# Keys turned by VectorE in square blocks and spread through DRAM, their product with V in three column tiles, from unit 3 on

## The chip, the cores and the metric

The kernel runs on one core of one Trainium2 chip (trn2). The metric is the device time of one execution in microseconds (us), lower is better. Five engines work side by side, each through its own instructions in their order: TensorE (PE; its weight loads are listed apart as PEld), VectorE (DVE), ScalarE (ACT), GpSimd (POOL) and SyncE (SP), which here issues all DMAs.

## The reference

Two stages stand one after the other. The first is linear attention with a complex decay per channel: for each of 4 batches and 8 heads a state S of 48 x 48 is carried over 768 time steps. The second takes the 3072 tokens of 384 numbers that come out and applies a two-layer network with the activation h * tanh(softplus(h)).

```python
B, H, S, D = 4, 8, 768, 48
for t in range(S):
    new_re = ar * S_re - ai * S_im
    new_im = ar * S_im + ai * S_re
    kv = np.einsum('bhd,bhe->bhde', k[:, :, t], v[:, :, t])
    S_re, S_im = (new_re + kv, new_im)
    y[:, :, t] = np.einsum('bhd,bhde->bhe', q[:, :, t], S_re)
...
h = x @ w_in                       # 384 -> 2048
g = h * np.tanh(softplus(h))
out = g @ w_out                    # 2048 -> 384
```

## The kernel before

The work is cut into 12 units of 256 tokens (`TU`), three for each batch, and a unit into two chunks of 128 time steps (`C`). Inside a chunk the recurrence is written as matrix products: with running products of the decay, q is multiplied by the growing product and k divided by it, each as a real and an imaginary part, so that a head has 96 rows (48 cosine, 48 sine).

**Elementwise stage** (`ew_steps`, L340). ACT, DVE and a few POOL instructions make the products of a unit; `rot` and `relay` (L498 to L507) send them by 12 DMAs a chunk (`T<-X`, `T<-QK`, L502) into the tile `T`, which has 96 partitions and for each of the 8 heads q, k and the end factor over the chunk's time. Three such tiles exist (`TB`).

**Attention stage** (`chunk`, L568), for each chunk:
- `kn` (L574): the keys of `T` are needed with time on the partitions. Eight TensorE transposes of 96 x 128 (L578, `pkn<-ident,T`) write PSUM, and two ACT copies (L579) bring them into `knat` (named `kn` in the profile), one buffer of 128 partitions, where the 96 columns of a head lie together and a column of zeros closes the tile. The last chunk of a batch has none, since its state is not carried on: 20 chunks of 24 turn their keys.
- `amat` (L582): keys times queries for each head, written from unit 3 on (`PU`) in two column tiles of 64 (L596); DVE masks the result into `am` (L599, L603).
- `yv` (L614): the output of the chunk, from the old state (`ypsum<-T,S`) and from `am` with V (`ypsum<-am,V`, and `ypsum<-am,vx` for a second copy of half of V whose partitions are swapped by halves, loaded at L377). L628 copies it to `y`, and `fin` (L673) sends `y` on by DMA (L676).
- `upd` (L633): keys times V for each head (L642, `pd<-V,kn`), in two column tiles of the array, channels 0 to 63 and 64 to 96 (the 97th is the zero column); then DVE adds the old state and multiplies by the end factor (L649, L650). It is left out where `kn` is.

These matmuls take float32 operands, and each is two hardware instructions in the profile; a transpose is one.

**Network stage** (`moe_steps`, L687). A unit has 8 steps `mm1` and 8 steps `mm2`. `mm1` (L709) makes 256 columns of h with 18 matmuls; then a chain of Exp, minimum, Square, Ln, Exp (L713 to L717) and `g` (L719) follows on ACT and DVE; g is split into a high part `gh`, a copy with a narrower type (L725, booked on the helper's L294, all on DVE here), and a low part `gl` (DVE, L295). `mm2` (L746) multiplies both into two output tiles with 12 matmuls.

**Order.** The order of each engine is written out by hand in the table `ORDER` (L73), as runs of instruction numbers, and `in_order` (L205) fixes it. What an engine does next, and also in which order SP issues its DMAs, is set by this table and not by a scheduler. An SP instruction that waits for a semaphore holds up all DMAs behind it.

Of the kernel before, what the change touches and what calls it, by code (L numbers as in the profile page):

```python
# [40 lines left out]
GACT = 0  # L41
# [14 lines left out]
WQ = 768  # L56
PU = 3
LW = [-15.9, -15.8, -15.7, -15.6, 2.0, 2.5, 3.0, 3.5, -2.0, -1.5, -1.0, -0.5, 5.0, 5.5, 6.0, 6.5]
# [70 lines left out]
    """,  # L129
    "DVE": """  # L130
# [89 lines left out]
def tile_kernel(ctx, tc, q, k, v, are, aim, w_in, w_out, out):  # L220
# [77 lines left out]
    nc.vector.memset(ypsum[32:64], 0.0)  # L298

    knat = at.tile([P, 2 * D * H + 1], F32, name="kn")  # L300
    nc.gpsimd.memset(knat[:, 2 * D * H:], 0.0)

    turned = []
    masked = []
# [696 lines left out]
```

## Time and profile before

| | |
|---|---|
| median of 3 runs | 594.03 us (592.22 to 594.89) |
| profiled execution, its own time | 596.8 us |
| span of its trace | 595.1 us |
| DVE busy | 482.4 us, 81% of the span |
| ACT busy | 476.6 us, 80% |
| POOL busy | 47.6 us, 8% |
| DMA | 68.9 MB, mean 116 GB/s |

The profile counts an engine busy while at least one of its instructions runs. Matmuls overlap each other, so the time that a matmul takes from the array is read from the distance of the starts and not from its own duration. The rows on TensorE stand in the prediction.

### The profile page before, as it was taken

To read this page: it belongs to the slowest core of one execution; us is meant where nothing else is said; L and a number is where in the kernel's file an instruction comes from. 1 tells how busy PE (TensorE), PEld (TensorE's weight loads), DVE (VectorE), ACT (ScalarE), POOL (GpSimd) and SP (SyncE) were. 2 spreads that over 40 slices of the span, in tenths; PEclk is the share of its full clock that TensorE was granted. 3 is DMA by queue.
4 is the path that set the end of the run, shared out by engine and by line. 5 is a ranking of instruction groups with operands and counts; after the bars stand their busy time and mean duration, and the time that the engine had idled before them with its cause. 6 is when DMAs were issued, how large, how long until landed. Compare 5 with 4: busy or idle time off the path is not lost.

```text
span 595.1 us, 12998 instructions
## 1 busy us (share of the span) xinstructions
PE 562.9 (95%) x5134; PEld 522.0 (88%) x5134; DVE 482.4 (81%) x890; ACT 476.6 (80%) x743; POOL 47.6 (8%) x58
## 2 busy tenths in 40 slices
PE   0989899989999999999999999999999999999995
PEld 0557687879998999999999899999999999999995
DVE  6999889999999897897796798797797787564553
ACT  7999889899987998798798798688797686546651
POOL 2102213170000000000010010000010010000000
PEclk9999899999999999999999999999999999999999
DMA  8788835715525608206407206417117115001001
GB/s 294 241 271 243 280 81 161 239 41 147 164 64 122 194 8 219 83 15 161 134 14 209 53 18 172 120 54 213 42 32 206 26 48 147 1 17 39 1 15 46
DMA packets 60421, 68.91 MB, mean 116 GB/s; under 512 B 5184, under 2 KB 53952, under 8 KB 60352
## 3 DMA queue, kind: packets, MB, share of 16 engines
q1 hardware_dynamic: 60352, 68.00, 39.7%
q8 instruction: 42, 0.69, 0.5%
q14 instruction: 27, 0.22, 0.1%
HBM read 38.73 MB, written 5.51 MB: 74 GB/s over the span
## 4 chain that ended last, share of the span: by engine, by line
PE 72%; DMA 8%; ACT 8%; DVE 6%; SPq 4%; issue 2%; DVEq 0%; ACTq 0%
PE po L746 28%; PE ph L709 28%; PE ypsum L623 5%; PE pa L596 4%; DMA T<-X 3%; SPq L502 2%; PE pd L642 2%; DMA raw<-w_out 2%; ACT e L262 2%; PE pkn L578 2%; ACT X L262 2%; ACT L270 1%; DMA T<-QK 1%; PE po L742 1%; DMA raw<-w_in 1%
## 5 line engine op out<-in xcount | busy, mean ns | idle before, releaser
L709 PE MATMUL ph<-xH,w 128*128 128x256 f32 x1104 | 230.5, 288 | 3.0 <-DVE g L719 2.9
L746 PE MATMUL po<-w,gh 128*128 128x384 f32 x704 | 205.5, 341 | 0.0
L709 PEld LDWEIGHTS ph<-xH,w 128*128 128x128 f32 x1104 | 182.4, 190 | 7.1 <-issue 2.1
L709 PE MATMUL ph<-xL,w 128*128 128x256 f32 x552 | 155.5, 283 | 0.5 <-DVE xL L295 0.5
L262 ACT ACTIVATE e<-e 128x512 f32<-128x512 f32 (+1 forms) x200 | 120.0, 609 | 20.8 <-DVE e L714 18.8
L746 PEld LDWEIGHTS po<-w,gh 128*128 128x128 f32 x704 | 128.7, 188 | 2.7 <-issue 1.3
L746 PE MATMUL po<-w,gl 128*128 128x384 f32 x352 | 118.8, 338 | 0.0
L709 PEld LDWEIGHTS ph<-xL,w 128*128 128x128 f32 x552 | 104.7, 190 | 2.1 <-DVE xL L295 0.8
L262 ACT ACTIVATE e<-ph 128x512 f32<-128x512 f32 (+1 forms) x100 | 57.2, 575 | 46.6 <-PE ph L709 41.1
L719 DVE SCALAR_TENSOR_TENSOR g<-e,ph 128x512 f32<-128x512 f32 (+1 forms) x100 | 65.8, 660 | 28.9 <-ACT e L262 23.0
L262 ACT ACTIVATE e<-e,fifth 128x512 f32<-128x512 f32 (+1 forms) x100 | 70.1, 702 | 1.8
L714 DVE TENSOR_SCALAR e<-e 128x512 f32<-128x512 f32 (+1 forms) x100 | 40.9, 411 | 32.9 <-ACT e L262 32.5
L746 PEld LDWEIGHTS po<-w,gl 128*128 128x128 f32 x352 | 66.2, 188 | 0.2
L270 ACT ACT_TABLE_LOAD x47 | 60.3, 1283 | 1.6 <-PEq L957 0.8
L295 DVE TENSOR_TENSOR gl<-g,gh 128x512 fp32r<-128x512 f32 x88 | 59.8, 685 | 0.7
L294 DVE CAST gh<-g 128x512 fp32r<-128x512 f32 x88 | 36.8, 420 | 6.6 <-PE po L746 5.7
L549 PE MATMUL junk<-cmask 128*128 128x512 bf16 x84 | 22.7, 416 | 15.7 <-DVE I L465 14.8
L262 ACT ACTIVATE X<-R 128x768 f32<-128x768 f32 (+1 forms) x40 | 29.6, 759 | 8.0 <-DVE R L442 5.3
L623 PE MATMUL ypsum<-am,V 128*48 128x128 f32 x240 | 35.6, 273 | 0.3 <-DVE am L610 0.2
L623 PE MATMUL ypsum<-T,S 96*48 96x128 f32 x320 | 34.2, 275 | 0.0
L323 POOL TENSOR_TENSOR raw<-raw 128x768 int32<-128x768 int32 x16 | 26.7, 1671 | 89.3 <-ACT raw L262 34.5
L262 ACT ACTIVATE X<-X 128x768 f32<-128x768 f32 (+1 forms) x42 | 31.3, 750 | 0.3
(91 smaller groups left out, 813.8 us busy)
## 6 DMA issues: line engine op xcount, KB each, us to landing
T<-X SPq DMA_DIRECT2D x72, 129.0 KB, 2.6
T<-QK SPq DMA_DIRECT2D x72, 129.0 KB, 2.6
raw<-w_in SPq DMA_DIRECT2D x8, 768.0 KB, 7.1
raw<-w_out SPq DMA_DIRECT2D x8, 768.0 KB, 6.3
V<-v SPq DMA_DIRECT2D x12, 384.0 KB, 4.2
out_dram<-o SPq DMA_DIRECT2D x24, 192.0 KB, 2.5
I<-a_im SPq DMA_DIRECT2D x11, 384.0 KB, 4.7
R<-a_re SPq DMA_DIRECT2D x11, 384.0 KB, 5.5
```

The lines of the kernel that those rows point to most:

```text
L262: ins = nc.scalar.activation(out, in_, func, **kw)
L270: ins = nc.scalar.preload_act_table_set(name)
L294: heng(h, src)
L295: leng(out=lo, in0=src, in1=h.bitcast(F32), op=ALU.subtract)
L323: nc.gpsimd.tensor_tensor(hi, hi, lo, ALU.add)
L549: ins = nc.tensor.matmul(junk, cmask, cmask.unsqueeze(1).broadcast_to([P, 4, P]), start=True, stop=True)
L596: nc.tensor.matmul(pa[row:row + C // 2, i, hi * C // 2:], T[:, 1, hi * C // 2:][:, :C // 2], T[:, 0, hi * C // 2:C], start=True, stop=True)
L623: nc.tensor.matmul(py[64 * par:64 * par + D, i, :], lhs, rhs, start=n == 0, stop=first or n == 1)
L709: nc.tensor.matmul(ph[:, a, :], rows_in(parts[j][:, wp], kt, a), st[xp][:, kt, :], start=n == 0, stop=n == 8)
L714: nc.vector.tensor_scalar_min(e, e, math.exp(20.0))
L719: nc.vector.scalar_tensor_tensor(g, e, 2.5, ph, ALU.subtract, ALU.mult)
L746: nc.tensor.matmul(po[t], gp[:, a, tsl], rows_out(parts[NPAIR + j][:, wp], a), start=j in starts and a == 0 and n == 0, stop=j + 1 in ends ...
```

## The change

**Keys, from unit 3 on (`KU`), in the 15 chunks that carry their state on.** `kn` is replaced by two steps. `kturn` is one DVE instruction that transposes the keys of all heads in blocks of 32 x 32 into a tile of 96 partitions by 1024 numbers; this tile lies in a buffer `idle()` that it shares with `vx`. `kspread` writes that tile to DRAM with one DMA (393 KB) and reads it back with three, one for each block of 32 channels, so that time lies on 128 partitions; a run is 256 numbers, 1 KB. `knat` then holds the channels as three groups of 32, each with all heads, and is still one buffer.

**Product with V.** `upd` has three column tiles of 32 channels (24 matmuls, 48 hardware instructions) from unit 3 on, where it had tiles of 64 and 33 (16 matmuls, 32 instructions).

**`vx`** has one buffer instead of two, since the space beside it is the new tile's.

**`gh`.** From unit 2 on, the copy for the steps 1, 3, 5 and 7 (`GA`) is made by ACT (`scalar.copy`) and not by DVE: 40 copies.

**Order.** The table `ORDER` is new for all engines.

```diff
-GACT = 0
+KU = 3
+GA = (1, 3, 5, 7)
...
     "PE": """
-        0+20 40+4 48+4 44+4 52+4 20+4 56+24 24+16 80+4 124+12 84+9 136+4 188+3 93+3 156+16 191+3 226+3 248+6 229+3
...
+        0+24 40+4 48+8 44+4 56+8 24+8 64+16 32+4 124+4 36+4 128+8 80+12 188+3 226+3 92+4 248+3 191+3 229+3 136+4 251+3
...
+    spare = []
+
+    def idle():
+        if not spare:
+            spare.append(wts.tile([P, 2 * WQ], F32, tag="w", name="vx", bufs=2 * NPAIR + 1))
+        return spare[0]
...
-            if not crossed:
-                crossed.append(wts.tile([P, 2, NCH, DM], F32, tag="w", name="vx", bufs=2 * NPAIR + 1)[..., :DM // 2])
-            st["vx"] = crossed[0][:, u % 2]
+            st["vx"] = idle()[:, :NCH * DM // 2].rearrange("p (c x) -> p c x", c=NCH)
...
+            def ktile():
+                return idle()[:2 * D, NCH * DM // 2:][:, :H * C]
+
+            def kturn():
+                kt = ktile().rearrange("p (b h k) -> p h b k", b=C // 32, h=H)
+                nc.vector.transpose(kt, st["T"][c][:, :, 1, :C].rearrange("p h (b t) -> p h b t", t=32))
+
+            def kspread():
+                kd = dram.tile([2 * D, H * C], F32, name=f"kd{u}_{c}")
+                nc.sync.dma_start(kd, ktile())
+                for a in range(2 * D // 32):
+                    nc.sync.dma_start(knat[:, a * 32 * H:(a + 1) * 32 * H],
+                                      kd[a * 32:(a + 1) * 32].rearrange("p (b x) -> b p x", b=C // 32))
...
-                pd = bank([2 * D + 1, H, D], "pd", "pd", c)
+                pd = bank([2 * D + (u < KU), H, D], "pd", "pd", c)
...
-                    for lo, hi in ((0, 64), (64, 2 * D + 1)):
-                        nc.tensor.matmul(pd[lo:hi, h, :], knat[:, h * 2 * D + lo:h * 2 * D + hi], own(c, h),
+                    for lo, hi in ((0, 64), (64, 2 * D + 1)) if u < KU else ((0, 32), (32, 64), (64, 96)):
+                        at0 = h * 2 * D + lo if u < KU else lo * H + h * 32
+                        nc.tensor.matmul(pd[lo:hi, h, :], knat[:, at0:at0 + hi - lo], own(c, h),
...
-            return ([] if last else [kn(0), kn(1)]), [amat(0), amat(1)], [take, yv(0), yv(1)], [] if last else [take, upd]
+            return ([] if last else [kn(0), kn(1)] if u < KU else [kturn, kspread]), [amat(0), amat(1)], [take, yv(0), yv(1)], [] if last else [take, upd]
...
-                split(g, gh, gl, nc.scalar.copy if unit < GACT else nc.vector.tensor_copy, nc.vector.tensor_tensor)
+                split(g, gh, gl, nc.scalar.copy if 1 < unit < UNITS and j in GA else nc.vector.tensor_copy, nc.vector.tensor_tensor)
```

Three places show how the new order reads. The first is TensorE's row before, in unit 5, chunk 0: the eight transposes stand between the network's matmuls (`po`, `ph`).

```order
L746 MATMUL po<-w_1630,gh 128x384 x2
L746 MATMUL po<-w_1630,gl 128x384
L578 MATMUL pkn<-ident,T 128x96 x8
L746 MATMUL po<-w_1093,gh 128x384
L746 MATMUL po<-w_1093,gl 128x384
```

In the changed kernel no transpose stands on TensorE from unit 3 on. The same chunk's product of keys and V there has its new form, 24 matmuls of 32 channels, and is followed at once by `yv`:

```order
L723 MATMUL ph<-xL,w_984 128x256
L723 MATMUL ph<-xH,w_984 128x256
L656 MATMUL pd<-V,kn 32x48 x24
L636 MATMUL ypsum<-T,S 48x128 x2
L636 MATMUL ypsum<-am,V 48x128
L636 MATMUL ypsum<-am,vx 48x128
```

Over the whole program, from the first `mm1` of split parts on, TensorE passes 78 times between the network's matmuls and those of `amat`, `yv` and `upd` before, and 68 times after. Of the 30 ends of the 15 new `upd` runs, 20 lie against `amat` or `yv`, the others against the network's matmuls. From the start of a unit's `amat` for chunk 0 to the start of its `upd` stand between 64 (unit 8) and 180 (unit 3) matmuls of the network.

The third place is SP's row in unit 3 of the changed kernel. `kd` is the tile in DRAM (3_0 is unit 3, chunk 0), `kn` is `knat`, `T<-X` and `T<-QK` are the relays for unit 4, and `xf<-y` sends unit 3's output on.

```order
L590 DMA kd_0_1730<-vx 96x1024
L365 DMA QK<-q 128x6x128
L376 DMA vx<-v 64x2x192 x2
L592 DMA kn<-kd_0_1730 128x1x256 x3
L590 DMA kd_1_1876<-vx 96x1024
L592 DMA kn<-kd_1_1876 128x1x256 x3
L501 DMA T<-X 16x8x258 x4
L501 DMA T<-QK 16x8x258 x3
L690 DMA xf<-y 128x1x256 x2
```

The write waits for `kturn`, the reads for the write's landing and for the `upd` that last read `knat`; relays and output stand behind them in the same queue.

More of the change, by code (lines that the diff above doesn't have):

```diff
@@ L130 @@
     "DVE": """
[29 rows of a table removed]
[29 rows of a table added]
     """,
     "Activation": """
[22 rows of a table removed]
[23 rows of a table added]
     """,
     "Pool": """
-        11+2 8 1 3 13 10 0 4 2 9 14+8 24 5 23 22 25+4 7 29 6 31+3 30 34 39 35 37 36 38 40+2 54 43 42 44+4 49 48 51 50
-        53 52
+        12+2 0 8 1 11 2+3 9 5+2 14 10 15+7 23 22 24+6 7 31 33 32 54 30 35 34 36+4 41 40 42+4 47 46 48+2 51 50 52+2
     """,
     "SP": """
[11 rows of a table removed]
[13 rows of a table added]
     """,
@@ L301, in tile_kernel @@
     nc.gpsimd.memset(knat[:, 2 * D * H:], 0.0)
+    spare = []
[3 more added lines that the diff above has]
+        return spare[0]
     turned = []
     masked = []
-    crossed = []
     def load_w(n):
```

224 rows, old and new, of the table ORDER are left out of this document.

## The prediction

> **What bounds the kernel now.** I read the page's first part, then the stretches, then the order of time on TensorE.
>
> ```profile
> PE 562.9 (95%) x5134; PEld 522.0 (88%) x5134; DVE 482.4 (81%) x890; ACT 476.6 (80%) x743; POOL 47.6 (8%) x58
> ```
>
> TensorE leads, but a share of the span doesn't say in which stretch. The busy time by stretches does (columns: stretch and its length, then busy time and instructions of each engine, granted clock, DMA share, GB/s):
>
> ```profile
> 0.00:30.00 30.00, 13.93 (x102) 7.76 (x103) 24.80 (x51) 25.74 (x47) 5.06 (x16) 1.00 0.80 267
> ...
> 120.00:150.00 30.00, 28.44 (x240) 26.40 (x238) 30.00 (x49) 29.19 (x46) 10.52 (x7) 1.00 0.32 93
> 150.00:200.00 50.00, 49.60 (x470) 47.82 (x468) 46.68 (x92) 43.94 (x66) 0.89 (x5) 1.00 0.50 140
> 200.00:250.00 50.00, 50.00 (x487) 48.54 (x486) 42.09 (x76) 43.34 (x65) 1.01 (x3) 1.00 0.43 113
> 250.00:300.00 50.00, 49.39 (x512) 47.68 (x511) 41.18 (x78) 41.73 (x63) 0.64 (x2) 1.00 0.32 92
> ```
>
> From 150 us on, where units 3 and later have their attention, TensorE is busy for 49.4 to 50 of 50 us at the full clock, while DVE and ACT have 3 to 9 us to spare. So there the end is set by how much array time the instructions take, one for one, and the change takes array time away. Before 150 us DVE and ACT are nearly full too; of the change only the order and four copies of unit 2 touch that part.
>
> **Transposes removed.** The timeline around unit 5's eight transposes (start, length, instruction):
>
> ```profile
> 238.40 0.34 PE L746 MATMUL po<-w,gl 128*128 128x384 f32 x1
> 238.58 0.82 PE L578 MATMUL pkn<-ident,T 96*128 96x96 f32 x8
> 239.19 0.42 PE L746 MATMUL po<-w,gh 128*128 128x384 f32 x1
> 239.44 0.34 PE L746 MATMUL po<-w,gl 128*128 128x384 f32 x1
> ```
>
> The next matmul starts 0.61 us after them, and its successor 0.25 us later where the usual distance is 0.17 (238.40 to 238.58): 0.61 + 0.08 = 0.69 us. Fifteen chunks lose them: 15 x 0.69 = **-10.4 us**. Their 30 copies on ACT go too.
>
> **The product with V** goes from 32 to 48 hardware instructions.
>
> ```profile
> 252.72 1.07 PE L642 MATMUL pd<-V,kn 128*64 128x48 f32 x31
> 253.58 0.31 PE L623 MATMUL ypsum<-T,S 96*48 96x128 f32 x1
> ```
>
> Its groups, weight loads (PEld) apart (busy us, mean ns of one, idle before):
>
> ```profile
> L642 PE MATMUL pd<-V,kn 128*64 128x48 f32 x320 | 22.2, 223 | 0.0
> ...
> L642 PEld LDWEIGHTS pd<-V,kn 128*64 128x64 f32 x320 | 20.7, 138 | 2.8 <-issue 2.1 <-ACT e L262 0.4
> ...
> L642 PE MATMUL pd<-V,kn 128*33 128x48 f32 x320 | 19.5, 213 | 0.0
> ...
> L642 PEld LDWEIGHTS pd<-V,kn 128*33 128x33 f32 x320 | 17.7, 110 | 0.0
> ```
>
> A run takes 253.58 - 252.72 = 0.86 us, 27 ns an instruction. If instructions come one after another at that distance, 48 take 1.29 us: +0.43 a chunk, +6.5 us in all. If column tiles run beside each other (one lasts 223 ns and the next starts long before its end), each tile has 16 instructions at 0.86 / 16 = 54 ns, and a tile of 33 columns has loads of 110 ns for 138 with 64: some 28 ns less, so 16 x 26 = 0.42 us with three tiles abreast, -0.44 a chunk, -6.5 us. A third tile would have to cost nothing for that. I take the middle, **0**, by which the third tile's cost and the shorter loads cancel, and keep both ends.
>
> **Changes of width.** Going between the network's matmuls, as wide as the array, and narrow tiles costs something:
>
> ```profile
> 279.41 0.28 PE L709 MATMUL ph<-xL,w 128*128 128x256 f32 x1
> 279.53 0.28 PE L709 MATMUL ph<-xH,w 128*128 128x256 f32 x1
> 279.74 1.56 PE L596 MATMUL pa<-T 96*64 96x128 f32 x32
> 281.23 0.45 PE L746 MATMUL po<-w,gh 128*128 128x384 f32 x1
> 281.51 0.34 PE L746 MATMUL po<-w,gl 128*128 128x384 f32 x1
> ```
>
> The first narrow one comes 0.21 us after its forerunner instead of 0.12, and after the run the second wide one comes 0.28 us after the first instead of 0.17: 0.09 in, 0.11 out, 0.10 a change. The new order has 68 such changes for 78: **-1.0 us**. Against this, 20 ends of the new `upd` runs now lie against `amat` or `yv`, a change from 32 to 64 columns which the trace doesn't have; between 0 and 0.10 each, 0 to 2.0 us; I take the middle, **+1.0**.
>
> The Trainium skill, "TensorEngine Tiling (Array Packing)", section "Tiling Modes", says that another tiling mode, and not merely another tile, drains the array. The rows above agree for full width against 64 columns; for 32 against 64 no row shows it. By that rule the term would be 2.0 instead of 1.0.
>
> **What moves to other engines.**
>
> ```profile
> L294 DVE CAST gh<-g 128x512 fp32r<-128x512 f32 x88 | 36.8, 420 | 6.6 <-PE po L746 5.7
> ...
> L579 ACT COPY kn<-pkn 128x384 f32<-128x384 f32 x40 | 18.5, 470 | 6.3 <-PE pkn L578 6.2
> ...
> L442 DVE TENSOR_TENSOR_SCAN R<-rmask,R 128x768 f32<-128x768 uint8 x10 | 17.5, 1747 | 0.1
> ...
> L412 DVE TENSOR_TENSOR X<-X 128x768 f32<-128x768 f32 x10 | 9.5, 950 | 0.0
> ...
> L294 ACT CAST xH<-xf 128x768 fp32r<-128x768 f32 x11 | 9.1, 827 | 3.3 <-DMA xf<-y 3.3
> ...
> L437 DVE TENSOR_SCALAR X<-X 128x768 f32<-128x768 f32 x10 | 5.5, 552 | 0.0
> ...
> L294 ACT CAST xH<-xf 128x384 fp32r<-128x384 f32 x2 | 0.9, 507 | 0.0
> ```
>
> A copy of 512 columns on ACT lies between 507 (384 columns) and 827 ns (768): 614. ACT gains 40 x 0.614 and loses 30 x 0.470: +24.6 - 14.1 = +10.5 us, one us in a unit. DVE loses 40 x 0.420 = 16.8. A block transpose isn't in the trace; 1024 numbers a row at the rates of L437 and of L442 are 0.74 and 2.33 us, and I take the rate of L412, the commonest for one result a number: 1.27 us, fifteen times 19.0. So DVE gains 2 us. Both hide behind TensorE, which the stretches allow from 150 us on: **0**. In unit 2 four copies, 2.5 us, go onto an ACT with 29.19 of 30 us taken, while DVE, with 30.00 of 30, is relieved of 1.7: between -1.7 and +2.5, taken as 0.
>
> **The way of the keys.** No engine's time, but a wait that was not there. Rows for its steps: DMAs with KB each and us to landing, then an issue's time on SP (least, median, most ns).
>
> ```profile
> T<-X SPq DMA_DIRECT2D x72, 129.0 KB, 2.6
> ...
> V<-v SPq DMA_DIRECT2D x12, 384.0 KB, 4.2
> ...
> R<-a_re SPq DMA_DIRECT2D x11, 384.0 KB, 5.5
> ...
> held<-o SPq DMA_DIRECT2D x4, 192.0 KB, 2.5
> ```
>
> ```profile
> L377 SPq DMA_DIRECT2D vx<-v x18: 556/600/815, 174.0 to 483.8; - x18
> ```
>
> Turn 1.27, issue 0.6, write 2.5 to 5.5 (a smaller write to DRAM; a load of its size), three reads issued 1.8, the last landed 2.6 to 4.2 later (one of its size; a load of all three's): 8.8 to 13.4 us, where transposes and copies took 0.69 and 0.47. What covers it in TensorE's new order is the `amat` run (1.49 us above) and then 64 to 180 network matmuls at 0.12 (L709) or 0.17 us (L746). For chunk 0 of units 3 to 11 that sums to 27.5, 16.4, 15.3, 12.2, 13.3, 10.4, 10.9, 13.5 and 11.6 us. For the write no end is the nearer (one row has the direction, the other the size), so I take 3.9, for the reads the row of their size: 10.2 us, which just fits under all nine, **0**. At 12 us three units wait, 1.6 + 1.1 + 0.4 = 3.1 us; at 13.4 it is 8.6. For chunk 1, only the reads are left after chunk 0's `upd` has released `knat`: 1.8 + 2.6 = 4.4 us under 6.6 or more. The largest wait of SP's queue (us in total, times, longest):
>
> ```profile
> SPq L762 <- DVE o L761: 99.4, 9, 25.9
> ```
>
> Sixty added DMAs, 36 us of SP, lie in such waits; behind a waiting read the next unit's relays stand, and they are late if the array reaches the next `amat` first.
>
> **Start.** TensorE's longest wait after the first 30 us (in brackets, with what ended it):
>
> ```profile
> 63.15 0.85 PE L578 MATMUL pkn<-ident,T 96*128 96x96 f32 x8 [2.03 <-DMA T<-X]
> ```
>
> Units 0 and 1 are only reordered; I bound what that gives or takes by this wait, 2.0 us either way, and take **0**.
>
> **Sum.** -10.4 + 0 - 1.0 + 1.0 + 0 + 0 + 0 = -10.4 us. The profiled execution took 596.8 us, 1.7 more than its span, so its like would take 586.4. The median of the runs is 594.03, 0.5% under the profiled one; less 10.4 it gives **583.6 us**.
>
> **Rivals.**
> 1. *The third tile costs as the others do.* The 27 ns an instruction hold, and `upd` takes +6.5 us: 583.6 + 6.5 = 590.1. For it speaks that 32 instructions took just 27 ns each; against it, that the narrower tile's loads are shorter and that instructions overlap eightfold (223 / 27). The Trainium skill, "TensorE: Matmul & The Clock Gate", section "Back-to-back issue gap", gives a floor of about 60 cycles, some 25 ns, to a matmul of 1 to 64 columns; by it an estimate for 48 is 1.2 us a run, 588.7 in all, and the trace's 27 ns agree with it without proving it.
> 2. *Three tiles abreast.* 0.42 us a run: 583.6 - 6.5 = 577.1.
> 3. *ACT becomes the bound.* Its +10.5 us land on the path: 594.1, no change. For it: ACT is at 43.9 of 50 us, and in a chain whose steps wait for each other. Against it: from 120 to 150 us TensorE did 28.44 of 30 with ACT at 29.19.
> 4. *The keys come late: slower.* One place, `upd` of chunk 0 waiting for `knat`. If the write takes as a 384 KB load (5.5), the reads too (4.2), and `kturn` stands behind a DVE instruction of 1.75 us (L442) in the queue, the way is 13.4 + 1.7 = 15.1 us. Then units 6 to 11 miss 2.9, 1.8, 4.7, 4.2, 1.6 and 3.5 us, 18.7 in all: 602.3. It eats the gain from about 13.7 us on.
>
> **How the numbers follow.** Forecast, 579 to 589: 0.54. Rival 1: 0.14; rival 2: 0.08; rival 3: 0.11; rival 4: 0.13. A measurement of this kernel can tell about 0.5%, 3 us, from no change. Faster, under 591.1: forecast, rival 2 and two thirds of rival 1, 0.72; within 0.5%: the rest of rival 1, rival 3 and mild lateness, 0.17; slower: 0.11. The range takes in rivals 1 to 3 and leaves out most of rival 4: 577 to 597.
>
> **What would show it.** The `pd` runs of 24 matmuls: 0.86 us, or 0.42 or 1.29. No wait of TensorE for DMA `kn` over a few tenths, none of `amat` for `T`. TensorE still at 49 to 50 of 50 us from 150 us on, and the last `po` some 10 us earlier. ACT near 487 us, DVE near 484. Wrong would be a row of waits `pd` for `kn` (rival 4), or TensorE with holes after `g` (rival 3).

## The result, and the profile after

The changed kernel takes **601.44 us** (median of 4 runs, 600.37 to 603.00), the kernel before 593.91 (4 runs, 592.22 to 594.89): ratio 1.0132, 95% interval 1.0100 to 1.0164. It is slower by 1.3%. The prediction was 583.6 with a range of 577 to 597, so it was wrong by 17.8 us, in sign and beyond the range. The profiled execution took 601.4 us with a span of 599.6.

The row of TensorE from the page after, and the same stretches as before (stretch, length, busy time and instructions of each engine, granted clock, DMA share, GB/s):

```profile
PE 555.0 (93%) x5254; PEld 513.8 (86%) x5254; DVE 480.8 (80%) x865; ACT 484.3 (81%) x753; POOL 38.2 (6%) x58
```

```profile
150.00:200.00 50.00, 47.41 (x484) 45.14 (x481) 44.47 (x78) 39.05 (x61) 1.02 (x2) 1.00 0.52 150
200.00:250.00 50.00, 46.57 (x476) 44.48 (x475) 40.58 (x74) 41.81 (x62) 0.42 (x2) 0.93 0.54 148
250.00:300.00 50.00, 47.51 (x478) 46.20 (x479) 44.86 (x81) 44.30 (x68) 0.93 (x4) 0.99 0.55 147
```

Where TensorE was busy for 49.4 to 50 us it now is for 46.6 to 47.5, and the granted clock is below 1 in two of the three stretches. TensorE has holes, and its largest waits behind the start (us in total, times, longest) name them:

```profile
PE pd L656 <- DMA kn<-kd: 8.3, 9, 1.5
PE pkn L577 <- DMA T<-QK: 5.4, 3, 2.4
PE ph L723 <- DVE g L733: 2.6, 3, 1.5
PE ypsum L636 <- DVE am L616: 2.4, 1, 2.4
```

The product of keys and V waits for the keys nine times; the second row lies in the units before 3, as before. The longest hole, at 222.9 us, is the fourth row, a wait for `am` and not for keys. VectorE had `am` behind an instruction that waited for ScalarE, and ScalarE waited for the load `I` (each engine's timeline, in brackets the idle time and what ended it):

```profile
222.84 1.76 DVE L484 TENSOR_TENSOR QK<-QK,X 128x1536 f32<-128x1536 f32 x1 [5.31 <-ACT R L278]
```

```profile
218.82 0.85 ACT L258 ACTIVATE X<-I 128x768 f32<-128x768 f32 x1 [2.94 <-DMA I<-a_im]
```

SyncE issued that load at 213.40, between a chunk's first and second read; the first read had held the queue until 212.79, when the write of its keys had landed. So this hole too stands behind the keys' hold on the queue. (In the run below whose reads don't wait for their write, a hole of 2.0 us is left there, so that wait alone doesn't make it.) Around it the stretches are:

```profile
224.00:225.00 1.00, 0.00 (x0) 0.00 (x0) 0.97 (x3) 0.00 (x0) 0.00 (x0) 0.50 0.00 0
225.00:226.00 1.00, 0.70 (x6) 0.60 (x8) 0.94 (x4) 0.00 (x0) 0.00 (x0) 0.50 0.00 0
226.00:228.00 2.00, 2.00 (x13) 1.63 (x10) 1.97 (x3) 1.90 (x4) 0.00 (x0) 0.50 0.25 89
228.00:230.00 2.00, 2.00 (x8) 2.00 (x7) 1.95 (x4) 1.97 (x4) 0.00 (x0) 0.50 0.30 108
```

Within a microsecond of the stop the granted clock falls to 0.5, and it stays there after the work is back. Two such stretches, 6.83 us at 223.8 and 3.41 us at 298.9, lie behind unit 3 in the trace after, none before. Compared by the distance of neighbouring starts, class by class, from 150 us on TensorE loses some 17.1 us in waits where it lost 3.7, and 4.3 us at half clock where it lost nothing: 17.7 us more. The waits for keys (8.3 us) and the one for `am` (2.4) are most of these waits.

Other rows that answer to the prediction's, from the groups by line of the kernel after (busy us, mean ns of one, idle before):

```profile
L290 ACT CAST gh<-g 128x512 fp32r<-128x512 f32 x40 | 24.4, 611 | 7.5 <-PE po L760 5.7 <-DVE g L733 1.6
L586 DVE STREAM_TRANSPOSE vx<-T 96x1024 f32<-96x1024 f32 x15 | 18.5, 1235 | 0.3 <-DMA T<-QK 0.2
```

And the run of unit 5, chunk 0, in TensorE's timeline after:

```profile
258.17 0.28 PE L723 MATMUL ph<-xH,w 128*128 128x256 f32 x1
258.37 0.88 PE L656 MATMUL pd<-V,kn 128*32 128x48 f32 x48
259.19 0.43 PE L636 MATMUL ypsum<-T,S 96*48 96x128 f32 x4
```

The two estimates of durations, 614 ns and 1.27 us, were near (611 and 1235 ns). The run with its end takes 259.19 - 258.37 = 0.82 us with 48 instructions, where 32 took 0.86: its 48 starts lie within 0.67 us, so the tiles do run abreast.

### The profile page after: what moved, and what is told of

Its sections match the earlier page's. It is cut to its first block, busy times and chain, and to the rows that moved or that the text cites. A ratio compares the mean times of both kernels' runs of the same rounds, so it can differ in the third digit from the quotient of the medians.

```text
span 599.6 us, 13309 instructions
## 1 busy us (share of the span) xinstructions
PE 555.0 (93%) x5254; PEld 513.8 (86%) x5254; DVE 480.8 (80%) x865; ACT 484.3 (81%) x753; POOL 38.2 (6%) x58
## 2 busy tenths in 40 slices
DMA packets 68041, 80.71 MB, mean 135 GB/s; under 512 B 5604, under 2 KB 60132, under 8 KB 67972
## 4 chain that ended last, share of the span: by engine, by line
PE 45%; DMA 19%; ACT 13%; DVE 13%; SPq 5%; issue 3%; DVEq 0%; ACTq 0%
PE po L760 17%; PE ph L723 15%; DMA kn<-kd 6%; ACT e L258 5%; DMA kd<-vx 5%; PE ypsum L636 4%; ACT X L258 2%; PE pa L609 2%; SPq L501 2%; PE pd L656 2%; PE junk L548 2%; PE ph L719 2%; PE po L756 2%; ACT L266 1%; SPq L592 1%
## 5 line engine op out<-in xcount | busy, mean ns | idle before, releaser
L723 PE MATMUL ph<-xH,w 128*128 128x256 f32 x1104 | 226.7, 287 | 2.6 <-DVE g L733 2.6
L760 PEld LDWEIGHTS po<-w,gh 128*128 128x128 f32 x704 | 130.3, 190 | 3.3 <-issue 1.8
L636 PE MATMUL ypsum<-am,V 128*48 128x128 f32 x240 | 37.0, 276 | 2.8 <-DVE am L616 2.4
L548 PE MATMUL junk<-cmask 128*128 128x512 bf16 x84 | 22.7, 418 | 14.4 <-DVE I L464 14.4
L324 POOL TENSOR_TENSOR raw<-raw 128x768 int32<-128x768 int32 x16 | 28.0, 1749 | 86.9 <-DVE raw L322 25.1
L656 PEld LDWEIGHTS pd<-V,kn 128*32 128x32 f32 (+2 forms) x880 | 18.0, 115 | 14.6 <-DMA kn<-kd 8.2
```

What stands on the lines that cost most here:

```text
L324: nc.gpsimd.tensor_tensor(hi, hi, lo, ALU.add)
L548: ins = nc.tensor.matmul(junk, cmask, cmask.unsqueeze(1).broadcast_to([P, 4, P]), start=True, stop=True)
L636: nc.tensor.matmul(py[64 * par:64 * par + D, i, :], lhs, rhs, start=n == 0, stop=first or n == 1)
L656: nc.tensor.matmul(pd[lo:hi, h, :], knat[:, at0:at0 + hi - lo], own(c, h), start=not on_pe, stop=True)
L723: nc.tensor.matmul(ph[:, a, :], rows_in(parts[j][:, wp], kt, a), st[xp][:, kt, :], start=n == 0, stop=n == 8)
L760: nc.tensor.matmul(po[t], gp[:, a, tsl], rows_out(parts[NPAIR + j][:, wp], a), start=j in starts and a == 0 and n == 0, stop=j + 1 in ends ...
```

## The experiments

Theory 1: the gain is there, and the late keys take more than all of it. Rival 2: the new order, or ACT and DVE with their added work, set the end. Theories under 1 (1a to 1j) differ in what makes the keys late. Each time is a median, beside the kernel before measured with it (594 to 595 us); the ratio to it has its 95% interval in brackets.

### What the way costs, and whether SyncE's queue is at fault

**No way at all.** The DMAs of `kspread` are left out; the order is that of the changed kernel without them.

```diff
             def kspread():
-                kd = dram.tile([2 * D, H * C], F32, name=f"kd{u}_{c}")
-                nc.sync.dma_start(kd, ktile())
...
+                return
```

> The changed kernel without the 60 transfers of the keys (15 writes to DRAM, 45 reads back); the block transposes on VectorE stay. From unit 3 on the product of keys and V uses the keys that unit 2 left in its buffers, so it is not that of the reference. Theory 1, the keys come late: the 10 us of waits for keys before the product and most of the 4.4 us at half clock go, 586 to 591 us, and no row of the waits names the keys. Rival 2, the new order, or ScalarE and VectorE with their added copies, set the end: 598 to 602 us, the time at which the product waited is waited elsewhere. Between 592 and 597 both have a part.

580.3 us, 0.978 (0.972 to 0.984). Better than either theory's figure: the way costs 601.4 - 580.3 = 21 us (by the two intervals, give or take 4), and the rest of the change gains 14. ACT is busy for 484.0 us here and DVE for 480.3, as in the changed kernel; they don't set the end, nor does the new order.

**The same transfers from GpSimd's queue.** Both calls of `nc.sync` in `kspread` become `nc.gpsimd`.

> The changed kernel with the 60 transfers of the keys issued by GpSimd on its own queue, at the same times as near as its program allows, and not by SyncE between the other transfers. Theory 1a, the keys are late because they stand in SyncE's queue behind transfers that wait and behind loads of 384 KB: the way from turn to landing falls from 15 to 17 us towards 10 us, 590 to 596 us. Rival 1b, the DMA engines themselves are what is shared, so the queue doesn't matter: 599 to 603 us. Rival 2 (new order, ScalarE, VectorE): 598 to 602 us, with fewer waits for keys.

667.6 us, 1.123 (1.116 to 1.130), far outside both. The reason is in GpSimd's timeline (start, length, instruction, in brackets the idle time ahead of it and what ended it):

```profile
167.37 0.68 POOL L589 DMA_DIRECT2D kd<-vx  x1 [0.35 <-DVE vx L585]
171.90 0.69 POOL L591 DMA_DIRECT2D kn<-kd  x1 [3.85 <-DMA kd<-vx]
176.17 0.69 POOL L591 DMA_DIRECT2D kn<-kd  x1 [3.57 <-issue]
180.13 0.68 POOL L591 DMA_DIRECT2D kn<-kd  x1 [3.28 <-issue]
```

The second and third read wait for nothing that the profile shows, yet each is issued 4 us behind the one before it, so the way became longer. TensorE waits for keys for 61.1 us in all. This says nothing of SyncE's queue, only that GpSimd's is no substitute here.

**Loads moved behind the reads**, 42 of them, in SyncE's row of `ORDER` alone; in unit 3:

```diff
-L365 DMA QK<-k 128x6x128
...
-L358 DMA I<-a_im 128x768
...
 L590 DMA kd_0_1730<-vx 96x1024
-L365 DMA QK<-q 128x6x128
-L376 DMA vx<-v 64x2x192 x2
 L592 DMA kn<-kd_0_1730 128x1x256 x3
+L365 DMA QK<-k 128x6x128
+L358 DMA I<-a_im 128x768
 L590 DMA kd_1_1876<-vx 96x1024
 L592 DMA kn<-kd_1_1876 128x1x256 x3
+L365 DMA QK<-q 128x6x128
+L376 DMA vx<-v 64x2x192 x2
```

> The changed kernel with 42 loads of R, I, Q, K and V that stood on SyncE up to four places ahead of a write of keys, or between it and its last read, put right behind that last read; nothing else moves. Theory 1a, the loads ahead in the queue make the keys late: the 10 us of waits for keys falls to 2 to 4 us, 592 to 597 us. Rival 1b, the way itself is too long even with a free queue: 600 to 603 us. Rival 3, the loads now come late in their turn: waits for I, R or V take the place of those for keys, 600 to 605 us.

652.0 us, 1.099 (1.092 to 1.106). TensorE's waits:

```profile
PE ypsum L636 <- DMA vx<-v: 26.5, 3, 14.2
PE ph L723 <- DVE g L733: 14.5, 2, 13.8
...
PE pd L656 <- DMA kn<-kd: 3.4, 3, 1.6
```

The waits for keys fall as theory 1a wants, but rival 3 takes their place, at 652 us where it had 600 to 605. In the longest wait the first chunk's `upd` starts at 468.9 us; the second chunk's keys are written at 471.9 and read from 475.0 on, `vx` stands behind these reads and is issued at 477.3, and the first chunk's `yv`, which needs `vx`, stops TensorE until 484.4. The run doesn't decide about the queue, since its loads were moved too far.

**Three column tiles alone**, in the kernel before.

```diff
...
-                    for lo, hi in ((0, 64), (64, 2 * D + 1)):
-                        nc.tensor.matmul(pd[lo:hi, h, :], knat[:, h * 2 * D + lo:h * 2 * D + hi], own(c, h),
+                    for lo, hi in ((0, 64), (64, 2 * D + 1)) if u < 3 else ((0, 32), (32, 64), (64, 96)):
+                        at0 = h * 2 * D + lo if u < 3 else h // 4 * 8 * D + lo * 4 + h % 4 * 32
+                        nc.tensor.matmul(pd[lo:hi, h, :], knat[:, at0:at0 + hi - lo], own(c, h),
```

> The kernel before with only the product of keys and V changed from unit 3 on to three column tiles of 32; the keys are turned on TensorE as before and ScalarE's copy lays them out in groups of 32. From the spans of the changed kernel: 48 instructions in 0.68 us against 32 in 0.86 us, 15 times, is 2.7 us less, and twenty borders between tiles 32 and 64 wide at 0.14 us is 2.8 us more, so 594 us, 592.5 to 595.5. Rival: the 0.18 us is only the modelled end of the matmuls and the borders alone remain, 596 to 598 us. Rival: the borders were hidden and only the gain remains, 591 to 592 us.

594.4 us against 594.7, 0.9985 (0.9956 to 1.0014): no difference, as expected. The shorter runs and the dearer borders cancel within the interval, which is 2.6 us down and 0.8 up.

### One trip, or no wait for the write

**One trip.** The blocks go straight from the turned tile to `knat`, without DRAM.

```diff
-                nc.sync.dma_start(kd, ktile())
...
+                    for b in range(C // 32):
+                        nc.sync.dma_start(knat[b * 32:(b + 1) * 32, a * 32 * H:(a + 1) * 32 * H],
+                                          ktile()[a * 32:(a + 1) * 32, b * 32 * H:(b + 1) * 32 * H])
```

> The changed kernel with the keys' way in one trip: no DRAM, each of the twelve square blocks of 32 rows by 256 columns (32 KB) goes from the turned tile straight to its place in the keys' buffer, twelve transfers of SyncE at the place of the old write. Theory 1c, what costs the 21 us is the second trip with its wait in SyncE's queue (reads that hold the queue until the write has landed, 38.9 us in 13 waits): turn to landing becomes about 12 issues of 0.62 us and 3 us, near 10.5 us, and the time 582 to 590 us. Rival 1d, any way through SyncE's queue is too long, since its instructions wait in order for other things: 597 to 603 us. Rival 1e, twelve small transfers take more of the queue than four: over 603 us.

628.6 us, 1.053 (1.045 to 1.061): rival 1e. SyncE's row for one chunk:

```profile
168.55 7.58 SPq L589 DMA_DIRECT2D kn<-vx  x12
176.17 0.62 SPq L363 DMA_DIRECT2D QK<-q  x1
```

Twelve issues hold the queue for 7.6 us, and all else on it is later; the queue's time is a price of its own. TensorE waits for `kn` no more here, but for `vx`, `am`, `g`, `y` and others.

**Reads that don't wait for this chunk's write.**

```diff
+    kds = []
...
                 kd = dram.tile([2 * D, H * C], F32, name=f"kd{u}_{c}")
+                kds.append(kd)
                 nc.sync.dma_start(kd, ktile())
+                kd = kds[max(len(kds) - 2, 0)]
```

> The changed kernel with all its 60 transfers, but each read takes the DRAM tile that the chunk before wrote, which has long landed; so the product uses the keys of the chunk before and is not that of the reference. The traffic, the queue and the order stay, only the wait for this chunk's write goes. Theory 1c, the wait for the write is the cost: 581 to 589 us, with less than 2 us of waits for keys. Rival 1f, the traffic of 12 MB and the places in the queue cost: 595 to 602 us.

596.2 us, 1.001 (0.997 to 1.005): rival 1f. Only 5.3 of the 21 us go (7 by the ratios), and the product still waits for `kn`, 5.4 us in five waits, although what is read had landed long before.

### Writes, reads, places, and the cut

**Better places in the queue**, done with more care than above: no `vx` moves, nor what waits on an `upd`. (The order that ran moved eleven loads, at ten chunks.)

> The changed kernel with only SyncE's order touched at eleven chunks: nine loads of R, I, Q, K and V of 384 KB that stood between a write of keys and its last read go behind that read, the three reads stand together, and the write of unit 7's second chunk goes ahead of the output and xf transfers that held it for 7 us. The loads of V's second copy and all that waits on the product of keys keep their places. Theory 1g, the places in SyncE's queue make the keys late: waits for keys fall from 10 us to 3 to 5 us, 590 to 596 us. Rival 1h, the queue has no better place, what is moved is late in its turn: 599 to 606 us.

602.3 us, 1.010 (1.006 to 1.015): rival 1h. In unit 6, where the changed kernel issues the reads 6.6 us behind the write, they now stood 3.9 behind it, and still TensorE waited for `kn` 6.3 us in all and for `am` 3.4. So these better places don't help, and the theory of the places falls as far as this order tests it.

**Only the writes, only the reads.** One kernel keeps the 15 writes and drops the reads, the other keeps the 45 reads and one write.

> The changed kernel with the 15 writes of turned keys but none of the 45 reads; from unit 3 on the product of keys and V uses the keys that unit 2 left in its buffer, so it is not that of the reference. If the 16 us that are left without the wait for the write are those of the reads (their issue, their landing behind loads, the wait for the one buffer): 580 to 584 us. If SyncE's wait for the turned keys ahead of each write, 25 us in 6 waits, holds other transfers back: 588 to 594 us.

> The changed kernel with the 45 reads of keys at their places, all from the DRAM tile that unit 3's first chunk wrote, and none of the other 14 writes; so the product uses the keys of one chunk and is not that of the reference. If the reads make the cost: 590 to 597 us, within 3 us of the run in which each read took the chunk before's tile. If the writes do: 581 to 586 us.

582.7 us, 0.979 (0.975 to 0.982), and 591.2, 0.994 (0.990 to 0.998). Above the 580.3 without any way, the writes alone cost 2.3 us and the reads alone 10.9. Those are 13.2 of the 21; the other 8 need both, and the run in which no read waits for this chunk's write puts 5.3 us on that wait. Such differences join runs whose kernel before lay between 593.9 and 595.4 us, so a cost of 2 us is not clear of noise.

**The two trips cut the other way:** three writes, one read.

```diff
-                kd = dram.tile([2 * D, H * C], F32, name=f"kd{u}_{c}")
-                nc.sync.dma_start(kd, ktile())
+                kd = dram.tile([C, 2 * D * H], F32, name=f"kd{u}_{c}")
                 for a in range(2 * D // 32):
-                    nc.sync.dma_start(knat[:, a * 32 * H:(a + 1) * 32 * H],
-                                      kd[a * 32:(a + 1) * 32].rearrange("p (b x) -> b p x", b=C // 32))
+                    nc.sync.dma_start(kd[:, a * 32 * H:(a + 1) * 32 * H].rearrange("(b p) x -> p b x", p=32),
+                                      ktile()[a * 32:(a + 1) * 32].rearrange("p (b x) -> p b x", b=C // 32))
+                nc.sync.dma_start(knat[:, :2 * D * H], kd)
```

> The changed kernel with the same two trips cut the other way: three writes of 128 KB and one read of 384 KB in rows of 3 KB at the place of the first read, instead of one write and three reads. SyncE's queue holds as many instructions. If the last read's place and landing (up to 8 us behind its issue) make the keys late, one read at the first one's place comes earlier: 592 to 598 us. If the first trip and the queue ahead of it set the time: 600 to 606 us.

**584.0 us** against 595.4, 0.981 (0.978 to 0.984): far better than expected, and faster than both kernels, with the same bytes and the same number of transfers. Two stretches show why. Both begin as a chunk's keys start to be read and no other transfer is under way, unit 9, chunk 1; first the changed kernel, then this one:

```profile
442.00:446.50 4.50, 4.50 (x36) 4.50 (x34) 4.34 (x11) 4.47 (x7) 0.00 (x0) 1.00 0.26 86
```

```profile
425.40:427.90 2.50, 2.50 (x19) 2.50 (x18) 2.44 (x6) 2.08 (x3) 0.00 (x0) 1.00 0.51 157
```

In the changed kernel the DMA share is 0.26 for all that time: 0.26 x 16 = 4.2, so some four engines carry all three reads, at 86 GB/s. The packets count the same thing. The DMA rows of the pages before, after and of this run:

```profile
DMA packets 60421, 68.91 MB, mean 116 GB/s; under 512 B 5184, under 2 KB 53952, under 8 KB 60352
```

```profile
DMA packets 68041, 80.71 MB, mean 135 GB/s; under 512 B 5604, under 2 KB 60132, under 8 KB 67972
```

```profile
DMA packets 69061, 80.72 MB, mean 139 GB/s; under 512 B 6144, under 2 KB 60672, under 8 KB 68992
```

Before, 324 transfers leave 5184 packets under 512 B, 16 each. Sixty more make 384 x 16 = 6144 in this run. After has as many transfers and only 5604, which is 339 x 16 + 45 x 4: each read of keys leaves four. The trace's marks of completion (steps of the semaphore that a transfer raises) agree: each of the 45 reads has five, one of them a microsecond behind its issue and four as its data lands, and all other transfers have sixteen. That made the last theory.

**The old write, the reads cut by partitions.** This keeps the one write, the runs of 1 KB and their number, and has more reads, not fewer.

```diff
-                for a in range(2 * D // 32):
-                    nc.sync.dma_start(knat[:, a * 32 * H:(a + 1) * 32 * H],
-                                      kd[a * 32:(a + 1) * 32].rearrange("p (b x) -> b p x", b=C // 32))
+                for b in range(C // 32):
+                    nc.sync.dma_start(knat[b * 32:(b + 1) * 32, :2 * D * H].rearrange("p (a x) -> p a x", a=2 * D // 32),
+                                      kd[:, b * 32 * H:(b + 1) * 32 * H].rearrange("(a p) x -> p a x", p=32))
```

> The changed kernel with the same write of 384 KB and the same 384 runs of 1 KB read back, but cut into four reads of 32 partitions by three runs in place of three reads of four blocks of 32 partitions; the reads stand at the places of the old three. In the changed kernel 45 reads brought 180 small packets (5604 under 512 B on its page, where 324 transfers of 16 and 15 writes of 16 make 5424), so four each, and ran at 97 GB/s alone: the order of the blocks puts a read on 4 of the 16 DMA engines. Theory 1i, this is why the reads land late: with 32 partitions outermost all 16 engines carry them, the page shows 5184 + 75 x 16 = 6384 packets under 512 B, waits for keys fall under 2 us, and the time is 582 to 588 us although there are more instructions in the queue. Rival 1j, it was the number of reads or their rows of 1 KB, which the run with one read of 3 KB rows changed as well: 597 to 605 us.

**585.2 us**, 0.982 (0.975 to 0.989): theory 1i. The page's count and TensorE's wait:

```profile
DMA packets 68821, 80.72 MB, mean 139 GB/s; under 512 B 6384, under 2 KB 60912, under 8 KB 68752
```

```profile
PE pd L655 <- DMA kn<-kd: 0.5, 1, 0.5
```

6384 small packets, as foretold from 16 a transfer, and 8.3 us of waits become 0.5. With the same write, the same runs and one transfer more for each chunk, what changed is how many engines carry a read; so the cause is shown twice, here and by the run with one read.

## Why the prediction was wrong

**The step that failed** is in the way of the keys: "for the reads the row of their size: 10.2 us, which just fits under all nine, **0**". That row was `T<-X`, 129 KB in 2.6 us. The reads have its size but not its shape. In the order's rows `T<-X` is 16x8x258. A read of keys is 128x1x256 on the side of `knat`, but on the side of DRAM the kernel's text cuts it into four blocks of 32 rows (`"p (b x) -> b p x"`). The first ran on 16 DMA engines, the second on four. So three reads take 4.7 us (first to last packet) where nothing disturbs them; by the marks of completion a read lands 4.9 us behind its issue (median of 45), and the last of three 6.1. Unit 6, SyncE's timeline after (start, length of the issue):

```profile
282.97 0.33 SPq L590 DMA_DIRECT2D kd<-vx  x1
...
286.79 0.52 SPq L358 DMA_DIRECT2D I<-a_im  x1
287.36 1.50 SPq L371 DMA_DIRECT2D V<-v  x1
288.96 0.59 SPq L365 DMA_DIRECT2D QK<-k  x1
289.60 1.77 SPq L592 DMA_DIRECT2D kn<-kd  x3
```

and TensorE's:

```profile
297.90 0.24 PE L656 MATMUL pd<-V,kn 128*32 128x48 f32 x2 [1.22 <-DMA kn<-kd]
299.24 1.49 PE L656 MATMUL pd<-V,kn 128*32 128x48 f32 x46 [1.09 <-DMA kn<-kd]
```

The turn had begun at 281.70 and the last read landed at 299.2: 17.5 us where the prediction had 10.2, and 13.4 at most. Of these, 6.6 lie from the write's issue to the first read's, where it had 4.5: the write landed after 3.8 us, and the reads stood behind eight other issues in the queue, the last three of them loads of 384 KB. From the first read's issue to the last one's landing are 9.6 us, where it had 4.4 (in unit 9, chunk 1, where nothing else was under way, 6.6). So 5.2 of the 7.3 us too many are the reads' and 2.1 the queue's. Over all 15 chunks the way took 15.0 us (median), and 9.3 in the run with one read.

The Trainium skill, "DMA: Bandwidth & Descriptors", section "Why a DMA increments its semaphore by 16 and not by 1", has the rule that was missing: a transfer runs on the largest number of engines up to 16 that divides the slowest dimension of both its sides, and of a transfer that SyncE issues only those engines post their completion. Four blocks against 128 partitions make four; the four small packets of each read and the share of 0.26 agree, and so does the run whose reads have 32 partitions outermost (16 small packets each).

**The other steps.**
- *Transposes, -10.4.* They can't be timed apart from the product, its borders and the changes of width, for which the sum had 0 together. From the same matmul in the middle of unit 2's `mm1`, shortly before unit 3's attention (it starts at 166.8 us before and at 162.6 in the run with one read), to the start of the last `po` (588.1 and 573.7) pass 421.3 and 411.1 us, 10.2 less; in the run without any way 408.0 us, 13.3 less. The kernel with three tiles alone, where nothing was expected to change, has 418.1, so one trace can be off by 3 us. By the medians the gain without any way is 14.4 us, of which 3.4 to 4.7 lie ahead of that matmul, so 9.7 to 11.0 are left. The term holds, within these bounds.
- *The product with V, 0, and its borders, +1.0 - 1.0.* The sum of nothing was right, by other parts. A run's starts lie within 0.67 us, about 0.18 less. Going from `yv` into a run of narrow tiles takes 0.20 us where it took 0.05, and out of it 0.14 where it took 0.01 (median distances of neighbouring starts): some 0.14 us for each border between tiles of 32 and 64, 2.8 in all, above the upper end of 2.0. So the rule of the Trainium skill, "TensorEngine Tiling (Array Packing)", section "Tiling Modes", that a change of mode drains the array, fits 32 against 64 as well. The run of the three tiles alone shows the sum, not the parts. Rival 1 and rival 2, 6.5 us up and down, are out.
- *ACT and DVE, 0.* Right, by the run without the way; rival 3 is out.
- *Write, 3.9.* Right: the write lands 3.8 us behind its issue (median, 3.0 to 8.4) in the changed kernel and 3.7 in the run with four reads.
- *Chunk 1, "4.4 us under 6.6 or more".* Wrong by the same row of 2.6: three of the nine waits for keys are at a second chunk.
- *Start, 0 within 2.0.* Mis-sized: the same matmul of unit 2 starts 166.8 - 163.4 = 3.4 us earlier in the changed kernel. One trace and another of the same work differ by 1 us there (167.8 with three tiles alone, which has the old order). So that part of the gain came ahead of unit 3's attention, from the new order and perhaps unit 2's four copies, which no run tells apart.
- *The clock* had no term. The holes made it 4.3 us, a quarter of the loss.
- *The queue.* The prediction laid the sixty issues into waits that were there anyway, at no price, though it named the danger for the relays. SyncE's waits after have this row (us in total, times, longest):

```profile
SPq L592 <- DMA kd<-vx: 38.9, 13, 5.7
```

What stands behind such a read is late, as the load `I` ahead of the longest hole. The run without this wait puts 5.3 us on it.

**Rival 4**, keys late, 602.3 us, named the place and came within a microsecond of the time, but by another sum: it had 18.7 us of waits for keys at six first chunks, from a slow write (5.5 us), reads of 4.2 us and a turn kept waiting, each at its end, and 13% for that. The write took 3.8 us (median) and the last read 6.1. TensorE waited for keys for 8.3 us, three of the nine times at second chunks, and the rest of the loss was other waits and the clock, against a larger gain, 14.4 us for 10.4. The runs bear out its place; that its price came so near is luck.

**What stays open.** The way still costs 584.0 - 580.3 = 3.7 us in the better cut, of which 0.8 us is a wait for keys. The two intervals (0.978 to 0.984, 0.972 to 0.984) overlap, so it may be less; where the rest lies was not tried, nor was a second buffer for the turned keys. Why GpSimd's reads follow each other at 4 us is open too.

## What to carry to other kernels

Take a transfer's time from a row of its shape, not only of its size: which dimension stands outermost, on either side, can decide how many DMA engines carry it, and the profile's page shows that by its small packets for each transfer and by a DMA share that stays flat at a quarter. Where the last wait is a transfer's, first look at how it is cut, before its place in the queue or the number of trips: the same bytes in as many transfers were worth 17 us here. A wait of the bounding engine may cost more than its length, since the clock stays low after it.

## What the hardware did that was not expected

- Reads of 128 KB with four blocks outermost ran on four of 16 engines, three of them together at 86 GB/s; one read of 384 KB in rows of 3 KB reached 157 GB/s.
- Transfers issued from GpSimd's queue followed each other at 4 us without any wait between them that the profile shows; from SyncE's, at 0.6 us.
- The granted clock fell to 0.5 within a microsecond of the stop at 222.9 us, though TensorE had worked until then apart from a wait of 1.0 us a little earlier; the wait lasted 2.4 us and the low clock 6.83.
- Three column tiles of 32 gave 48 starts in 0.67 us, 14 ns apiece, where two wider tiles gave 27.
